# First MLP of a three-layer fused kernel: activations cast and split for two ff tiles at a time, second layer taken a pair of tiles behind

## The chip, the core and the metric

The kernel runs on one core of a Trainium2 chip. The metric is the device time of one execution in microseconds, the median of several. The engines are named as the profile names them: PE is the matrix engine (PEld its weight loads), DVE the vector engine, ACT the scalar engine, POOL the GpSimd engine, SP the engine that issues most DMAs.

## The reference

Inputs are q, k and v of shape (4, 8, 576, 64), a first MLP with d_model 512 and d_ff 1536, and a second one with d_ff 2048. Weights arrive as float64.

```python
A = sm(q, k_lm); Bm = sm(q_lm, k_lm); C = sm(q_lm, k)     # 32 landmarks, means of 18 rows
Z = ...                                                   # six Newton steps towards Bm's inverse
attn = A @ Z @ C @ v                                      # (4, 8, 576, 64) -> x of (2304, 512)
x = (sigmoid(x @ w_gate) * (x @ w_val)) @ w_out           # first MLP, d_ff 1536
h = x @ w_in                                              # second MLP, d_ff 2048
out = (max(h, 0) + alpha * min(h, 0)) @ w_out2            # (2304, 512) float32
```

## The kernel before, in words

There are four batches of 576 tokens. In each, the attention's right half (Z C v) is folded into the gate and value weights of the first MLP (`fold`, L590, and `take`, L609, make the tiles `We`), so that the first layer of the MLP multiplies the attention's left factor A directly with `We`.

Every fp32 product is made of three products of fp32r operands: an operand is split into a cast and a rest. `split` (L113) issues a cast on ACT (L115) and a subtraction, the rest, on DVE, or on POOL where asked (L116). `TERMS` (L57) lists the three products.

The first MLP works on a half batch (288 tokens, `HB`) and one ff tile (128 of 1536 columns) at a time. There are 4 x 2 x 12 = 96 such steps, walked by the loop at L756. A step calls `layer1` (L630): 6 matmuls of 288 columns into the bank gv0 (gate) and 6 into gv1 (value). ACT takes the sigmoid of gv0 into `g` (L649), DVE multiplies g by gv1 in place (L650), and `split` makes the cast and the rest of `g` in `gs` (L651). The result goes to the queue `behind` (L758). With `LAG = 2`, `catch_up` (L727) then takes the tile of two steps ago and calls `layer2` (L654): 4 output blocks of 128 columns x 3 terms = 12 matmuls of 288 columns, accumulated in four banks `acc` over a half's ff tiles. So PE's own order is: first layer of step n, second layer of step n-2, first layer of step n+1, and so on.

Where a half ends (its twelfth ff tile), the four banks are copied to four `xs` tiles, m = 0 and 2 on ACT, m = 1 and 3 on DVE (L746; in the first batch, whose halves are worked through in three segments of ff tiles, DVE adds a stored part, L744). SP stores each to DRAM (`x2d<-xs`, L748). There are eight such ends. The next half's `layer2` starts new accumulators in the same four banks.

Beside this loop run, in the same steps: conversions of the float64 weights (`narrow`, L124: ACT L130 and L134, DVE L136, L139, L142), for the second MLP from step 52 on (`narrow_w2`, L678); conversions of the stored second weights (`convert_w2`, L694); the attention of the next batches; the folds. Every engine takes its instructions in order. The framework lays that order down when the program is built, from the order of the code and its own modelled times, so instructions of neighbouring steps can change places on ACT and DVE. SP's queue also is in order: an issue that waits for a buffer holds up the issues behind it.

After step 96 the second MLP begins (L890): `layer3` (L828), and three steps later `layer4` (L850), with accumulators in the banks of `acc` and `att`. Each of its first steps also calls `catch_up` once while tiles of the first MLP are left in `behind` (L899). `store` (L862) copies a finished block into an `ob` tile, which uses the buffers of `gs`, and stores it.

Buffer counts (L63): `g` 2, `gs` (and `ob`) 4, `xs` 4.

Of the kernel before, what the change touches and what calls it, by code (L numbers as in the profile page):

```python
# [9 lines left out]
F32 = mybir.dt.float32  # L10
F32R = mybir.dt.float32r
# [10 lines left out]
def tile_landmark_attention_glu_prelu(  # L22
# [18 lines left out]
    P = 128  # L41
# [4 lines left out]
    HB = S // 2  # L46
# [5 lines left out]
    NW = 512  # L52
# [7 lines left out]
    RELOAD_AT, FOLD_AT = (16, 40), (  # L60
        (19, 20, 22, 23, 25, 27), (44, 46, 48, 50, 52, 54), (45, 47, 49, 51, 53, 55)
    )
    LAG, LAG2, G_BUFS, GS_BUFS, XS_BUFS = 2, 2, 2, 4, 4  # L63
    W2_OWN, W2_RAW = (0, 1), (29, 30, 31)
    W2_EARLY, W2_EVERY = 4, 2
    W2_FROM, W2_STEP, X2_AT = 85, 3, (11, 6)
# [6 lines left out]
    bpool = ctx.enter_context(tc.tile_pool(name="bpool", bufs=1))  # L73
# [28 lines left out]
    def f32(ap):  # L102
        return ap.bitcast(F32)
# [6 lines left out]
    def bank(name, tag="att"):  # L110
        return psp.tile([P, NW], F32, tag=tag, name=name, bufs={"att": 2, "gv": 2, "acc": 4}[tag])

    def split(dst, src, lo="dve"):  # L113

        nc.scalar.copy(dst[:, 0, :], src)  # L115
        (nc.gpsimd if lo == "pool" else nc.vector).tensor_tensor(  # L116
            out=dst[:, 1, :], in0=src, in1=f32(dst[:, 0, :]), op=ALU.subtract
        )
# [507 lines left out]
            split(We[B - 1, c, j], st, lo="pool")  # L626

    wout_sb = {}

    def layer1(b, half, f):  # L630
        c, s = divmod(f, 2)
        pss = []
        for i in range(2):
            ps = bank(f"gv{i}", "att" if b >= 2 and f % 2 else "gv")
            n = 0
            for a, e in TERMS:
                for j in range(2):
                    nc.tensor.matmul(  # L638
                        ps[:, :HB],
                        lhsT=We[b, c, j][:, a, 256 * i + P * s : 256 * i + P * s + P],  # L640
                        rhs=att[b, j, "A"][half][:, e, :],
                        start=(n == 0),
                        stop=(n == 5),
                    )
                    n += 1
            pss.append(ps)
        g = bpool.tile([P, HB], F32, tag="g", name="g", bufs=G_BUFS)
        gs = bpool.tile([P, 2, HB], F32R, tag="gs", name="gs", bufs=GS_BUFS)
        nc.scalar.activation(g, pss[0][:, :HB], AF.Sigmoid)  # L649
        nc.vector.tensor_tensor(out=g, in0=g, in1=pss[1][:, :HB], op=ALU.mult)  # L650
        split(gs, g)  # L651
        return gs

    def layer2(acc, gs, f, f0, f1):  # L654
        for m in range(NK):
# [69 lines left out]
    behind = deque()  # L725

    def catch_up():  # L727
        b, half, f, f0, f1, gs = behind.popleft()
        if f == f0:
            accs[half] = [bank(f"acc{m}", "acc") for m in range(NK)]  # L730
        layer2(accs[half], gs, f, f0, f1)
        if f < f1 - 1:
            return
        if f0 == 0 and f1 < NF1:
            part[half] = [ws_tile("part", (P, 2, HB), F32) for _ in range(2)]
        for m in range(NK):
            got, so_far = accs[half][m][:, :HB], None
            if f0 > 0 or f1 < NF1:
                so_far = part[half][m // 2][:, m % 2]
            to = so_far  # L740
            if f1 == NF1:
                to = bpool.tile([P, HB], F32, tag="xs", name="xs", bufs=XS_BUFS)
            if f0 > 0:
                nc.vector.tensor_tensor(out=to, in0=so_far, in1=got, op=ALU.add)  # L744
            else:
                (nc.vector.tensor_copy if m % 2 else nc.scalar.copy)(to, got)  # L746
            if f1 == NF1:
                nc.sync.dma_start(out=x2d[2 * b + half][:, m], in_=to)  # L748

    for b in range(B):  # L750
        if b == 0:
            segs = [(h, f0, f1) for f0, f1 in ((0, 2), (2, 6), (6, NF1)) for h in range(2)]
        else:
            segs = [(h, 0, NF1) for h in range(2)]
        order = [(h, f, f0, f1) for h, f0, f1 in segs for f in range(f0, f1)]
        for i, (half, f, f0, f1) in enumerate(order):  # L756
            at = 24 * b + i
            behind.append((b, half, f, f0, f1, layer1(b, half, f)))  # L758
            if len(behind) > LAG:
                catch_up()  # L760
            for _ in range(min(CPS, len(conv))):
                convert()
                raw_ahead(1)

            if b < 2:
                pace += ATT_PACE[b] * (at >= ATT_FROM)
                while pace >= 1:
                    next(nxt, None)
                    pace -= 1
            if at in RELOAD_AT:  # L770
                reload(0)
                reload(1)
            if at in FOLD_AT[0]:
                c = FOLD_AT[0].index(at)
                while (1, 1, "M") not in att:
                    next(nxt)
                take(1, c, fold(1, c, bank))
                reload(c + 2)
            if at in FOLD_AT[1]:
                c = FOLD_AT[1].index(at)  # L780
                for _ in nxt:
                    pass
                take(2, c, fold(2, c, bank))
            if at in FOLD_AT[2]:
                c = FOLD_AT[2].index(at)
                store_folded(c, fold(3, c, bank))
                reload(c + 2)
                if c + 1 == NCH:
                    apool.release()
                    qpool = ctx.enter_context(  # L790
                        tc.tile_pool(name="qpool", bufs=1, reuse_waits="tile")
                    )
                    rpool = tc.alloc_tile_pool(name="rpool", bufs=1, reuse_waits="tile")
            if b == 2 and half and f % 2:
                take_stored(f // 2)

            if at >= NARROW_FROM:
                narrow_pace += 1 / NARROW_EVERY
                while to_narrow and narrow_pace >= 1:
                    narrow_w2(to_narrow.popleft())  # L800
                    narrow_pace -= 1
            if qpool is not None and at > FOLD_AT[2][-1]:
                if at % W2_EVERY == 0:
                    if w2_todo and w2_todo[0] < W2_EARLY:
                        convert_w2(w2_todo.popleft())
                if at >= W2_FROM:
                    if w2_todo:
                        convert_w2(w2_todo.popleft())
# [50 lines left out]

    outv = out.rearrange("(b p r) e -> b r p e", b=B, r=R)  # L860

    def store(acc, n0, t):  # L862
        ob = bpool.tile([P, NW], F32, tag="gs", name="ob", bufs=GS_BUFS)
        (nc.vector.tensor_copy if t % 2 else nc.scalar.copy)(ob, acc)
        done = 0
        while done < P:
            bb, rem = divmod(n0 + done, S)
            r, p = divmod(rem, TP)
            step = min(P - done, TP - p)
            nc.sync.dma_start(out=outv[bb, r, p : p + step, :], in_=ob[done : done + step, :])  # L870
            done += step
# [67 lines left out]
```

## Time and profile before

| | |
|---|---|
| median of 3 runs | 899.93 us (895.19 to 902.99) |
| the profiled execution, its own time | 898.93 us |
| its span, first to last instruction | 897.1 us |
| mean granted clock of PE over the span | 0.972 of full speed |

The profile is of one execution. Busy time counts an instruction's duration on its engine; an engine's idle time before an instruction is put down to whatever released that instruction last. The first MLP's matmuls lie between 49 and 504 us of the span, the second MLP's from 495 us to the end. The granted clock has two levels, 1.2 and 2.4 GHz, shown as 0.5 and 1.

### The profile page before, as it was taken

The page shows a single profiled execution, that of the slowest core. Times are in us where ns is not written, and L with a number is a line of the kernel's source. Part 1 is how long each engine was busy: PE and PEld are TensorE (multiplying, and loading weights), DVE is VectorE, ACT ScalarE, POOL GpSimd, SP SyncE. Part 2 cuts the span into 40 slices and gives each one's busy share as a digit, 9 for nine tenths or more (in the row PEclk, how much of TensorE's full clock was granted, in tenths as well). Part 3 has the DMA queues.
Part 4 walks back from the last instruction along what each step waited for, and adds up shares of the span by engine and source line. Part 5 has one row for each costly group of instructions (what it writes and reads, how often), then busy time and mean ns, then how long its engine had stood idle before and what let it go on. Part 6 is the DMA issues. An engine that isn't in the chain of part 4 may idle for free.

```text
span 897.1 us, 15129 instructions
## 1 busy us (share of the span) xinstructions
PE 853.4 (95%) x5969; PEld 710.7 (79%) x5969; DVE 508.9 (57%) x1005; ACT 337.1 (38%) x711; POOL 92.4 (10%) x90
## 2 busy tenths in 40 slices
PE   5689889999999999998999999999999999999997
PEld 4357667877887877998999888888888888888896
DVE  3789998565565343778766664444344333443443
ACT  6666865354364333555555431121121111111111
POOL 0131112110011000133200020110010001000000
PEclk9679999999999999998999999999999999999999
DMA  9776778734331242888876530020002000100100
GB/s 248 247 221 177 253 240 257 216 115 135 81 104 49 94 145 94 271 282 253 265 250 194 153 86 21 16 78 1 1 24 58 1 1 13 48 0 1 31 18 24
DMA packets 85160, 106.92 MB, mean 119 GB/s; under 512 B 35664, under 2 KB 57184, under 8 KB 85088
## 3 DMA queue, kind: packets, MB, share of 16 engines
q1 hardware_dynamic: 81632, 93.36, 34.7%
q0 software_dynamic: 3456, 12.58, 4.5%
q8 instruction: 47, 0.77, 0.4%
q14 instruction: 25, 0.20, 0.1%
HBM read 78.65 MB, written 27.26 MB: 118 GB/s over the span
## 4 chain that ended last, share of the span: by engine, by line
PE 84%; DVE 6%; DMA 5%; issue 2%; ACT 2%; POOL 1%; SPq 0%; DVEq 0%; ACTq 0%
PE h L834 22%; PE o L852 22%; PE gv L638 15%; PE acc L657 14%; PE psf L600 4%; DMA raw<-in_moe_w_out_dram 2%; PE psq L191 2%; DMA raw<-in_moe_w_in_dram 1%; PE psc L210 1%; DVE raw L139 1%; PE psz L403 1%; PE psa L210 1%; DMA tk<-in_k_dram 1%; PE psv L314 1%; DMA tkT<-in_k_dram 1%
## 5 line engine op out<-in xcount | busy, mean ns | idle before, releaser
L638 PE MATMUL gv<-A,we 128*128 128x288 f32 x1152 | 197.8, 312 | 6.0 <-ACT g L649 3.4
L638 PEld LDWEIGHTS gv<-A,we 128*128 128x128 f32 x1152 | 167.1, 196 | 36.8 <-issue 25.6
L657 PE MATMUL acc<-gs,wconv 128*128 128x288 f32 x1152 | 184.5, 304 | 8.8 <-DVE xs L746 3.5
L834 PE MATMUL h<-x,w 128*128 128x512 f32 (+1 forms) x840 | 183.8, 368 | 0.0
L657 PEld LDWEIGHTS acc<-gs,wconv 128*128 128x128 f32 x1152 | 163.8, 192 | 20.8 <-issue 6.8
L852 PE MATMUL o<-w,g2s 128*128 128x512 f32 x702 | 170.0, 390 | 0.0
L834 PEld LDWEIGHTS h<-x,w 128*128 128x128 f32 x840 | 148.1, 188 | 27.2
L852 PEld LDWEIGHTS o<-w,g2s 128*128 128x128 f32 x702 | 130.9, 188 | 26.6
L115 ACT CAST g2s<-g 128x512 fp32r<-128x512 f32 (+1 forms) x80 | 46.3, 578 | 269.3 <-DVE g L844 269.3
L840 DVE TENSOR_SCALAR g<-h,alphaT 128x512 f32<-128x512 f32 (+1 forms) x80 | 55.8, 697 | 148.6 <-PE h L834 148.5
L116 DVE TENSOR_TENSOR g2s<-g,g2s 128x512 fp32r<-128x512 f32 (+1 forms) x80 | 55.7, 696 | 55.1 <-ACT g2s L115 54.5
L650 DVE TENSOR_TENSOR g<-g,gv 128x288 f32<-128x288 f32 x96 | 43.1, 449 | 39.2 <-PE gv L638 38.0
L649 ACT ACTIVATE g<-gv 128x288 f32<-128x288 f32 x96 | 39.5, 411 | 66.1 <-PE gv L638 62.9
L116 DVE TENSOR_TENSOR gs<-g,gs 128x288 fp32r<-128x288 f32 x96 | 52.0, 541 | 21.2 <-ACT gs L115 20.9
L115 ACT CAST gs<-g 128x288 fp32r<-128x288 f32 x96 | 41.5, 432 | 50.7 <-DVE g L650 50.4
L116 POOL TENSOR_TENSOR x<-xr,x 128x512 fp32r<-128x512 f32 (+1 forms) x20 | 23.9, 1206 | 314.1 <-ACT x L115 313.9
L139 DVE SCALAR_TENSOR_TENSOR raw<-raw 128x512 uint32<-128x512 uint32 x68 | 47.6, 711 | 13.0 <-ACT raw L134 12.2
L130 ACT ACTIVATE raw<-raw 128x512 f32<-128x512 f32 x68 | 46.2, 681 | 21.9 <-DMA raw<-in_moe_w_out_dram 9.5
L844 DVE SCALAR_TENSOR_TENSOR g<-h,g 128x512 f32<-128x512 f32 (+1 forms) x80 | 51.0, 638 | 2.6
L600 PE MATMUL psf<-wgv,m 64*32 64x512 f32 x384 | 43.4, 625 | 0.4 <-DVE m L469 0.2
L116 DVE TENSOR_TENSOR we<-psf,we 128x512 fp32r<-128x512 f32 x36 | 23.6, 686 | 18.6 <-ACT we L115 18.5
L115 ACT CAST we<-psf 128x512 fp32r<-128x512 f32 x36 | 19.8, 588 | 29.6 <-PE psf L600 29.5
(129 smaller groups left out, 735.1 us busy)
## 6 DMA issues: line engine op xcount, KB each, us to landing
raw<-in_moe_w_out_dram SPq DMA_DIRECT2D x28, 512.0 KB, 4.9
wgv<-wgvd POOLq DMA_DIRECT2D x24, 512.0 KB, 4.6
raw<-in_moe_w_in_dram SPq DMA_DIRECT2D x16, 512.0 KB, 3.9
w2d<-n SPq DMA_DIRECT2D x32, 256.0 KB, 2.6
st<-w2d SPq DMA_DIRECT2D x32, 256.0 KB, 2.9
raw<-in_moe_w_gate_dram SPq DMA_DIRECT2D x24, 256.0 KB, 4.6
raw<-in_moe_w_val_dram SPq DMA_DIRECT2D x24, 256.0 KB, 4.9
wgvd<-wgv SPq DMA_DIRECT2D x12, 512.0 KB, 5.6
```

The lines of the kernel that those rows point to most:

```text
L115: nc.scalar.copy(dst[:, 0, :], src)
L116: (nc.gpsimd if lo == "pool" else nc.vector).tensor_tensor(out=dst[:, 1, :], in0=src, in1=f32(dst[:, 0, :]), op=ALU.subtract)
L130: nc.scalar.activation(w[:, :, 1], w[:, :, 1], AF.Copy, scale=2.0 ** -112)
L139: nc.vector.scalar_tensor_tensor(out=lo, in0=hi, scalar=0x80000000, in1=lo, op0=ALU.bitwise_and, op1=ALU.bitwise_or)
L600: nc.tensor.matmul(pss[j][LM * h : LM * h + LM], lhsT=att[b, j, "M"][d, u], rhs=wgv[c, j][d, u], start=True, stop=True,)
L638: nc.tensor.matmul(ps[:, :HB], lhsT=We[b, c, j][:, a, 256 * i + P * s : 256 * i + P * s + P], rhs=att[b, j, "A"][half][:, e, :], start=(n ...
L650: nc.vector.tensor_tensor(out=g, in0=g, in1=pss[1][:, :HB], op=ALU.mult)
L657: nc.tensor.matmul(acc[m][:, :HB], lhsT=wout_sb[f][:, a, P * m : P * m + P], rhs=gs[:, e, :], start=(f == f0 and n == 0), stop=(f == f1 - ...
L834: nc.tensor.matmul(ps[:, :n], lhsT=w[:, a, kk], rhs=xs[:, e, kk, :n], start=(i == 0), stop=(i == 11))
L840: nc.vector.tensor_scalar(out=g[:, :n], in0=ps[:, :n], scalar1=0.0, scalar2=alphaT[:, f : f + 1], op0=ALU.min, op1=ALU.mult,)
L844: nc.vector.scalar_tensor_tensor(out=g[:, :n], in0=ps[:, :n], scalar=0.0, in1=g[:, :n], op0=ALU.max, op1=ALU.add)
L852: nc.tensor.matmul(acc, lhsT=gs[:, a, P * t : P * t + P], rhs=w2_out[f][:, e, :], start=(f == 0 and i == 0), stop=(f == NF2 - 1 and i == 2),)
```

## The change

`g` becomes a tile for two ff tiles. Sigmoid and product still run once per ff tile, each into its half. After the second tile of a pair, one `split` makes cast and rest of 576 columns into one `gs` tile of both. `layer1` therefore returns nothing at an even tile and two entries at an odd one, so that the second layer of a step is that of three steps ago, and three entries instead of two are left when the first MLP's loop ends. The buffer counts become `g` 2 (of twice the size), `gs` 2 (of twice the size), `xs` 3. Two `ob` tiles of the final store share one `gs` buffer.

```diff
-    LAG, LAG2, G_BUFS, GS_BUFS, XS_BUFS = 2, 2, 2, 4, 4
+    LAG, LAG2, G_BUFS, GS_BUFS, XS_BUFS = 2, 2, 2, 2, 3
...
+    both = [None]
...
-        g = bpool.tile([P, HB], F32, tag="g", name="g", bufs=G_BUFS)
-        gs = bpool.tile([P, 2, HB], F32R, tag="gs", name="gs", bufs=GS_BUFS)
+
+        if s == 0:
+            both[0] = bpool.tile([P, 2, HB], F32, tag="g", name="g", bufs=G_BUFS)
+        g = both[0][:, s]
         nc.scalar.activation(g, pss[0][:, :HB], AF.Sigmoid)
         nc.vector.tensor_tensor(out=g, in0=g, in1=pss[1][:, :HB], op=ALU.mult)
-        split(gs, g)
-        return gs
+        if s == 0:
+            return []
+        gs = bpool.tile([P, 2, 2, HB], F32R, tag="gs", name="gs", bufs=GS_BUFS)
+        split(
+            gs.rearrange("p a s t -> p a (s t)"), both[0].rearrange("p s t -> p (s t)")
+        )
+        return [(f - 1, gs[:, :, 0]), (f, gs[:, :, 1])]
...
-            behind.append((b, half, f, f0, f1, layer1(b, half, f)))
+            behind.extend((b, half, ff, f0, f1, gs) for ff, gs in layer1(b, half, f))
             if len(behind) > LAG:
                 catch_up()
...
+    out_tiles = [None]
+
     def store(acc, n0, t):
-        ob = bpool.tile([P, NW], F32, tag="gs", name="ob", bufs=GS_BUFS)
+        if t % 2 == 0:
+            out_tiles[0] = bpool.tile([P, 2, NW], F32, tag="gs", name="ob", bufs=GS_BUFS)
+        ob = out_tiles[0][:, t % 2]
```

## Rows read from the trace of the kernel before

**Rows 1.** The page's first part: busy time of each engine.

```profile
PE 853.4 (95%) x5969; PEld 710.7 (79%) x5969; DVE 508.9 (57%) x1005; ACT 337.1 (38%) x711; POOL 92.4 (10%) x90
```

**Rows 2.** By stretch: busy PE, PEld, DVE, ACT, POOL; granted clock, DMA share, GB/s.

```profile
50.00:200.00 150.00, 140.94 (x1258) 106.33 (x1258) 122.19 (x271) 91.83 (x198) 28.51 (x29) 0.96 0.72 212
...
350.00:500.00 150.00, 143.58 (x1023) 140.16 (x1022) 106.95 (x186) 80.39 (x170) 23.45 (x16) 0.95 0.74 239
```

**Rows 3.** What PE waited for, whole span: us in total, times, longest.

```profile
PE acc L657 <- DVE xs L746: 3.5, 3, 1.9
PE gv L638 <- ACT g L649: 3.4, 3, 2.3
PE acc L657 <- ACT xs L746: 3.0, 2, 2.3
...
PE acc L657 <- DVE gs L116: 2.1, 2, 1.6
```

**Rows 4.** Busy time by stretch around the three waits for xs; columns as in rows 2.

```profile
376.00:386.00 10.00, 8.62 (x53) 8.62 (x54) 7.42 (x14) 4.92 (x12) 2.63 (x3) 0.83 0.91 270
418.00:428.00 10.00, 8.14 (x38) 7.80 (x39) 7.65 (x15) 4.49 (x11) 1.26 (x1) 0.66 0.93 281
461.00:469.00 8.00, 6.37 (x33) 5.78 (x33) 6.65 (x14) 4.97 (x13) 0.00 (x0) 0.79 0.73 216
```

**Rows 5.** Groups by form, ACT casts and DVE rests of 288 and 576 columns.

```profile
L116 DVE TENSOR_TENSOR gs<-g,gs 128x288 fp32r<-128x288 f32 x96 | 52.0, 541 | 21.2 <-ACT gs L115 20.9
...
L115 ACT CAST gs<-g 128x288 fp32r<-128x288 f32 x96 | 41.5, 432 | 50.7 <-DVE g L650 50.4
...
L115 ACT CAST A<-at 128x576 fp32r<-128x576 f32 x6 | 4.1, 676 | 5.1 <-DVE at L362 5.1
...
L116 DVE TENSOR_TENSOR A<-at,A 128x576 fp32r<-128x576 f32 x4 | 3.0, 757 | 0.7 <-ACT A L115 0.7
...
L116 DVE TENSOR_TENSOR A<-at,A 128x288 fp32r<-128x288 f32 x4 | 1.7, 451 | 0.0
```

**Rows 6.** Timeline of an undisturbed step, third batch: start, duration, what, idle before.

```profile
357.35 1.74 PE L638 MATMUL gv<-A,we 128*128 128x288 f32 x12
...
360.15 0.46 DVE L116 TENSOR_TENSOR gs<-g,gs 128x288 fp32r<-128x288 f32 x1 [0.50 <-ACT gs L115]
...
365.29 0.95 PE L657 MATMUL acc<-gs,wconv 128*128 128x288 f32 x6
```

**Rows 7.** Timeline where a half of the third batch ends.

```profile
373.89 0.43 ACT L746 COPY xs<-acc 128x288 f32<-128x288 f32 x1
...
375.43 1.52 DVE L116 TENSOR_TENSOR gs<-g,gs 128x288 fp32r<-128x288 f32 x1
...
375.78 2.86 SPq L748 DMA_DIRECT2D x2d<-xs  x4
...
377.38 1.46 PE L657 MATMUL acc<-gs,wconv 128*128 128x288 f32 x9 [1.95 <-DVE xs L746]
```

**Rows 8.** The same where the third batch itself ends.

```profile
418.53 0.43 ACT L115 CAST gs<-g 128x288 fp32r<-128x288 f32 x1 [0.43 <-DVE g L650]
418.87 0.39 ACT L746 COPY xs<-acc 128x288 f32<-128x288 f32 x1
...
420.60 2.58 PE L657 MATMUL acc<-gs,wconv 128*128 128x288 f32 x9 [0.55 <-DVE xs L746]
```

**Rows 9.** DMAs of tile xs; the issue of 419.28 alone; that of 461.89 alone.

```profile
DMA to landing us min/median/max: 1.7/3.9/6.6
x2d<-xs SPq DMA_DIRECT2D x1, 144.0 KB, 3.8
x2d<-xs SPq DMA_DIRECT2D x1, 144.0 KB, 1.7
```

**Rows 10.** Timeline where the second MLP begins.

```profile
502.20 1.78 PE L657 MATMUL acc<-gs,wconv 128*128 128x288 f32 x12
...
505.48 0.81 DVE L746 COPY xs<-acc 128x288 f32<-128x288 f32 x2
```

## The prediction

> **What bounds the kernel now.** I read the page's busy line first, because it says which engine can set the end. PE is busy for 853.4 of 897.1 us [rows 1]; its work is untouched by this change, which alters ACT, DVE and buffers alone. So the question is where PE waits for those two. The table by stretch comes next [rows 2]. From 50 to 200 us PE is busy for 140.9 of 150 us, with DVE at 122.2 and ACT at 91.8. From 350 to 500 it has 6.4 us of idle time, at DVE 107 and ACT 80. From 500 on PE runs the second MLP, which this change leaves as it is but for its first steps.
>
> The list of waits names the causes [rows 3]: 3.4 us for the sigmoid, 2.1 us for the rest of `gs`, and 3.5 + 3.0 = 6.5 us for the copies `xs` out of the four accumulators. These last are the whole idle time of the third stretch. They lie at three places, the ends of halves near 377, 419 and 462 us. After each, the granted clock falls to its lower level for a time [rows 4]: a mean of 0.83 over 10 us is 3.4 us at 1.2 GHz, 0.66 is 6.8 us, 0.79 over 8 us is 3.4 us. That is 13.6 us at half speed, which costs about 6.8 us. So the three places together cost some 13 us, and from 50 to 200 us PE is idle for 150 - 140.9 = 9 us, of which 5.5 us are the waits for the sigmoid and the rest.
>
> **The change, part by part.**
>
> *One cast and one rest for two tiles.* The 96 casts of 432 ns become 48. A cast of 576 columns is in the trace, at 676 ns, so a pair saves 2 x 432 - 676 = 188 ns, or 9.0 us of ACT in all. The rest of 576 columns took 757 ns. Against two of 451 ns (undisturbed) a pair saves 145 ns; against two of the mean 541 it saves 325 ns. That is 7 to 16 us of DVE [rows 5]. Half or more of it falls where PE hardly waits, and of the saving from 50 to 200 us (some 13 pairs: 2.4 us of ACT, 1.9 to 4.2 us of DVE) only what shortens a queue that PE waits for counts. PE's idle time there is 9 us [rows 2], ended by these two engines in 5.5 us at the least [rows 3]. DVE's load falls by 2 to 3%, and since a queue that is nearly full shortens by more than its load, I give 13% of the 9 us back: -1.2 us. Bounds: -9 if all goes, and +1.5 if the longer instructions make the five waits of these two rows longer by 0.31 us each (757 - 451).
>
> *The second layer a pair behind.* Before, the rest of tile f is wanted after four blocks: second layer of f-2, first of f+1, second of f-1, first of f+2. After, from the odd tile's first layer to the even tile's second layer there are again four blocks, and six to the odd one's. From 357.35 to 365.29 there are five blocks, so a block is 1.59 us. In this undisturbed step the rest ends at 360.61 and its first reader starts at 365.29, so 4.7 us are to spare [rows 6]. Cast and rest of a pair end (676 - 432) + (757 - 451) = 0.55 us later. I cost this at 0; the cover is those 4.7 us, and if a late queue eats them each pair costs up to 0.55 us. The two `gs` buffers are free when wanted: the last reader of the pair before last stands one first-layer block, 1.59 us, ahead.
>
> *One more block of lag.* The first second-layer block starts one step later at the head, and three blocks instead of two are left for the second MLP. PE's sum is the same. If PE were starved at the head the moved block would cost its 1.59 us; from 50 to 200 us PE is idle for 6% only [rows 2], so I take +0.3 (0 to 1.6).
>
> *The accumulators at the end.* Before, the last second-layer block starts at 502.20 and the copies on DVE end at 506.29 [rows 10], beside a block of `layer3`. After, that block comes a step later and directly ahead of the first `layer4`, which wants two of the four banks. The copies' 4.1 us from the block's start, less the block's 1.6, are then uncovered if nothing is put between: 0 to 2.5 us. The other two accumulators of that step use other banks and another `layer3` stands ready, so I take +0.5.
>
> *Three xs tiles.* The fourth copy (m = 3, DVE) must now wait until the store of m = 0 has landed. Behind it on DVE stand the narrowing of weights, the rest of a converted weight and the next product; behind those wait ACT's cast, the free raw buffers and so SP's next loads. On an ideal schedule the block that ends a half starts at B, the copy of m = 0 is done at about B + 1.0 (three matmuls, 0.4, and the copy, 0.43), and the next half reaches its fourth accumulator at B + 2 x 1.59 + 1.19 (nine of twelve matmuls) = B + 4.37. So 4.37 - 1.0 - 0.45 = 2.9 us are there for issue and landing. The median landing is 3.9, the range 1.7 to 6.6 [rows 9]. In the first two batches folds and attention matmuls stand between the blocks and PE waited for no xs copy [rows 2, 3], so I count no place there. At the last end the fourth copy has no reader near. Three places remain:
>
> - 377 us: the first store is issued at 375.78, 1.46 us after its copy, since SP's queue was held [rows 7]; it landed about 3.8 us later, at 379.6. The fourth copy would end at 380.1 and its three matmuls at 380.5 or so, where the block ended at 378.84: +1.7.
> - 419 us: copied at 418.87, landed 3.8 us after the issue of 419.28, at 423.1. The block would end at about 424.1 instead of 423.18: +1.0 [rows 8, 9]. But the step in which a half ends is an even one now (the twelfth tile's second layer comes at the third step of the next half), and even steps have no cast and no rest. Here the copy stood behind a `gs` cast that itself waited 0.43 us for DVE's product [rows 8]. Without the cast, and with DVE's queue lighter by one rest, I take 1.6 us off: -0.6.
> - 462 us: landed after 1.7, before the fourth copy ran anyway: 0.
>
> Sum +1.1. Bounds: -13.3 if the lighter step takes the waits and the low clock away (6.5 + 6.8), and 3 x (6.6 - 2.9) = +11.1 with the longest landing at each place, issued at once.
>
> Two rules of the Trainium skill are weighed against this. The rows have DVE busy for 57% and ACT for 38% of the span [rows 1], and what they cost PE are waits in their queues [rows 3]. "Perfetto Trace Analysis", section on optimizing Scalar and DVE operations, says that grouping helps where the engine is saturated, but that where these engines are not and still cause bubbles on others, breaking instructions up may finish work sooner; by that the change goes the wrong way, which is the third rival below. The store's landing took 3.8 us at two of the three places [rows 9]. "DMA: Bandwidth & Descriptors", section on the anatomy of a DMA, gives about 2.0 us of fixed time; with that, 377 would add nothing, and the sum would be about -1.0 us.
>
> *The rest* (`ob` pairs, `g` of twice the size): a block's stores lie far apart, no wait of PE hangs on them, 0.
>
> Sum: -1.2 + 0 + 0.3 + 0.5 + 1.1 = +0.7 us against the profiled execution's 898.93, so 899.6. The median of the runs lies 1.0 above that execution, so I name 900.5.
>
> **Rivals.**
>
> 1. *Slower: the third xs buffer decides.* Where the store's issue is held as at 377 us and the landing takes 3.8, the fourth copy comes 5.3 us after the first, against the 2.9 that are covered; it decides once issue and landing pass 2.9. If all three places pay the 1.7 of 377 (5.1), the low clock lasts 6.8 us instead of 3.4 at two of them (2 x 1.7 = 3.4), and the end pays its 2.5, the sum is +11: 911. For it: the loads of SP stand ahead of the stores, and the DMA share there is 0.73 to 0.93 [rows 4]. Against it: at 462 the landing took 1.7, and the waits already there would be replaced, not added to.
> 2. *Faster: the lighter step ends the waits at the halves.* If the copies run as soon as their matmuls end, 6.5 us of waits and 6.8 of clock go, of which the store's landing gives part back. Half of it is -6.6: 893; all of it 887. For it: at 419 the cast stood in front of the copy, and at 377 a rest of `gs` of 1.52 us stood in front of DVE's copies [rows 7, 8]. Against it: the landing of the first store replaces the wait, and the narrowing of weights stays in the same queues.
> 3. *Bursts: the longer cast and rest hold up the sigmoid and the product.* In the first two batches the next first layer wants the banks back one block later. ACT is held 0.24 us longer and DVE 0.31 us longer at every second step. With the five waits of today it is +1.5 in place of -1.2, 2.7 over the forecast: 903; with all 24 pairs of those batches it is 24 x 0.31 = 7.4: 908. For it: PE's wait for the sigmoid is the longest of its kind today, 3.4 us [rows 3]. Against it: the two engines have less work in all.
>
> That the saving is hidden entirely lies inside the forecast: then the time is that of before.
>
> **How the numbers follow.** The forecast, between -3 and +4 us of before, gets 0.50; the first rival 0.18, the second 0.20, the third 0.12. A measurement of this kernel can tell about 1% from no change, 9 us. Below 891 lies a little less than half of the second rival: 0.09. Above 909 lies some two thirds of the first: 0.12. The rest, 0.79, is within. The range from 891 to 909 leaves out those two tails. Cases of both signs hold much of the chance; the forecast's own range is 897 to 904.
>
> **What would show it.** Groups by form should show 48 casts near 676 ns and 48 rests near 757 to 900 ns, and about 9 us less of ACT. The list of waits should show `acc <- xs` waits at the three places again, ended now by DVE's fourth copy, with the store's landing as that copy's own releaser, and still 2 to 4 us together more or less than 6.5. The granted clock should fall again near the same ends of halves. The sigmoid and `gs` waits up to 200 us should sum to about 8 us. I would be wrong if the waits for xs pass 10 us or vanish, if a new wait for `gs` appears in the second batch, or if the second MLP's first steps lose more than 2.5 us.

## The result, and the profile after

The changed kernel takes 907.91 us (median of 4 timed executions, 907.0 to 911.84) beside 898.76 us for the kernel before (895.19 to 902.99): a ratio of 1.0100, with a 95% interval of 1.0061 to 1.0139 (below, such an interval stands in brackets behind its ratio). It is slower, by about the 9 us that this measurement can just tell from no change. The profiled execution took 908.52 us with a span of 906.5 us, 9.4 us more than the 897.1 of before. In the listings below L639 is the matmul of `layer1`, L665 that of `layer2`, L754 and L756 the copies `xs` and their stores, L842 and L860 the matmuls of `layer3` and `layer4` (before: L638, L657, L746, L748, L834, L852).

The engines' part of the page, which answers to [rows 1], and the groups by form, which answer to [rows 5]:

```profile
PE 853.2 (94%) x5969; PEld 706.6 (78%) x5969; DVE 499.8 (55%) x957; ACT 329.9 (36%) x663; POOL 92.9 (10%) x90
```

```profile
L116 DVE TENSOR_TENSOR gs<-g,gs 128x576 fp32r<-128x576 f32 x48 | 37.2, 776 | 16.9 <-ACT gs L115 16.7
L115 ACT CAST gs<-g 128x576 fp32r<-128x576 f32 x48 | 32.3, 672 | 29.7 <-DVE g L653 28.4 <-PE acc L665 1.2
```

The change does what it says. ACT gives up 41.5 - 32.3 = 9.2 us of casts and DVE 52.0 - 37.2 = 14.8 us of rests. PE is as busy as before, and its idle time grew from 43.7 to 53.3 us (span less busy time). The equal sum hides something: up to the ninth block of `layer3` PE's busy time falls from 498.05 to 492.70 us, and from there to the end it grows from 355.36 to 360.49.

PE's waits, which answer to [rows 3] (us in total, times, longest), and the granted clock around the ends of halves, which answers to [rows 4] (the clock is third from the end):

```profile
PE acc L665 <- DVE xs L754: 7.9, 4, 3.7
PE gv L639 <- ACT g L652: 5.7, 5, 2.5
PE acc L665 <- ACT xs L754: 4.6, 2, 3.8
...
PE acc L665 <- DVE gs L116: 1.4, 3, 1.0
```

```profile
373.00:385.00 12.00, 8.28 (x59) 7.61 (x58) 10.11 (x16) 5.54 (x12) 2.01 (x2) 1.00 0.79 261
419.00:429.00 10.00, 8.18 (x41) 8.10 (x42) 6.98 (x14) 6.00 (x12) 3.65 (x2) 0.66 0.90 294
462.00:477.00 15.00, 11.23 (x62) 10.79 (x63) 8.52 (x17) 6.39 (x12) 0.00 (x0) 0.77 0.81 273
```

The waits for xs are 12.5 us where they were 6.5. The clock falls to its lower level at two of the three places, for 6.8 us each (a mean of 0.66 over 10 us, 0.77 over 15): 13.6 us in sum, as before. But 6 us more of waits are not 9.4. The table by stretch shows where the rest is: first the stretch from 540 us of the kernel before, then that of the one after, with the two that answer to [rows 2] ahead of it:

```profile
540.00:890.00 350.00, 350.00 (x1635) 293.49 (x1634) 148.04 (x224) 51.71 (x92) 13.12 (x12) 1.00 0.07 19
```

```profile
50.00:200.00 150.00, 136.26 (x1238) 103.38 (x1237) 120.28 (x252) 88.81 (x183) 27.52 (x28) 0.97 0.69 210
350.00:500.00 150.00, 138.32 (x981) 135.84 (x981) 99.92 (x162) 75.95 (x148) 24.35 (x16) 0.95 0.75 240
540.00:890.00 350.00, 350.00 (x1597) 288.73 (x1596) 145.23 (x215) 50.69 (x90) 13.14 (x12) 1.00 0.07 19
```

From 350 to 500 us PE is idle for 11.7 us, where it was 6.4. From 540 on, in the second MLP, which the change touches only in its first steps, PE has no idle time in either kernel, at a full clock, and does 1597 matmuls where it did 1635 (part of this difference is that the short matmuls at the end are reached later). Is each matmul slower? Here are the ninth and the eightieth block of `layer3` in the timeline (start, duration), before and after:

```profile
536.47 1.30 PE L834 MATMUL h<-x,w 128*128 128x512 f32 x5
...
886.13 1.11 PE L834 MATMUL h<-x,w2r 128*128 128x256 f32 x8
```

```profile
540.66 1.09 PE L842 MATMUL h<-x,w 128*128 128x512 f32 x4
...
895.41 1.36 PE L842 MATMUL h<-x,w2r 128*128 128x256 f32 x10
```

It is 4.2 us behind at the ninth block and 9.3 at the eightieth, so 5.1 us are lost between: this stretch takes 354.75 us in place of 349.66. The groups by form of the stretch from 560 to 860 us say which matmuls are slower (the last number ahead of the bar's 0.0 is the mean of one in ns), before and after:

```profile
L834 PE MATMUL h<-x,w 128*128 128x512 f32 x533 | 128.1, 389 | 0.0
L852 PE MATMUL o<-w,g2s 128*128 128x512 f32 x531 | 127.9, 389 | 0.0
...
L852 PE MATMUL o<-w2x,g2s 128*128 128x512 f32 x42 | 10.2, 390 | 0.0
L834 PE MATMUL h<-x,w2x 128*128 128x512 f32 x36 | 8.6, 389 | 0.0
```

```profile
L842 PE MATMUL h<-x,w 128*128 128x512 f32 x541 | 133.4, 394 | 0.0
L860 PE MATMUL o<-w,g2s 128*128 128x512 f32 x528 | 127.5, 390 | 0.0
...
L860 PE MATMUL o<-w2x,g2s 128*128 128x512 f32 x36 | 8.9, 395 | 0.0
L842 PE MATMUL h<-x,w2x 128*128 128x512 f32 x36 | 8.7, 390 | 0.0
```

`layer3` is slower with weights `w`, not with `w2x`; `layer4` is slower with `w2x`, not with `w`. From start to start a `layer3` matmul with weights `w` takes 229 and 237 ns by turns, 232.7 on average, in place of 227. What tells these apart is where the two operands lie. `x2` and `w2x` are in pools allocated behind `bpool`, `w` and `g2s` are not. The change makes `bpool` larger by two tiles `g` of 1152 bytes per partition and smaller by one `xs` of 1152, so everything behind it lies 1152 = 4 x 256 + 128 bytes higher. The slow matmuls are those of which one operand moved and the other didn't.

### The profile page after: what moved, and what is told of

It is laid out like the page before. It is cut to its first block, busy times and chain, and to the rows that moved or that the text cites. A ratio compares the mean times of both kernels' runs of the same rounds, so it can differ in the third digit from the quotient of the medians.

```text
span 906.5 us, 15024 instructions
## 1 busy us (share of the span) xinstructions
PE 853.2 (94%) x5969; PEld 706.6 (78%) x5969; DVE 499.8 (55%) x957; ACT 329.9 (36%) x663; POOL 92.9 (10%) x90
## 4 chain that ended last, share of the span: by engine, by line
PE 72%; DMA 11%; DVE 8%; ACT 3%; issue 3%; SPq 1%; POOL 1%; DVEq 0%; ACTq 0%; POOLq 0%
PE o L860 22%; PE h L842 21%; PE gv L639 10%; PE acc L665 9%; DMA raw<-in_moe_w_out_dram 4%; PE psf L600 3%; DMA st<-w2d 2%; DVE raw L139 2%; PE psq L191 2%; DMA st<-we3d 1%; DMA x2d<-xs 1%; PE psc L210 1%; DMA raw<-in_moe_w_in_dram 1%; PE psv L314 1%; DVE n L142 1%
## 5 line engine op out<-in xcount | busy, mean ns | idle before, releaser
L639 PE MATMUL gv<-A,we 128*128 128x288 f32 x1152 | 195.9, 309 | 10.4 <-ACT g L652 5.7
L665 PE MATMUL acc<-gs,wconv 128*128 128x288 f32 x1152 | 183.2, 303 | 13.9 <-DVE xs L754 7.9
L639 PEld LDWEIGHTS gv<-A,we 128*128 128x128 f32 x1152 | 164.5, 192 | 40.5 <-issue 24.1
L842 PE MATMUL h<-x,w 128*128 128x512 f32 (+1 forms) x840 | 187.9, 372 | 0.0
L665 PEld LDWEIGHTS acc<-gs,wconv 128*128 128x128 f32 x1152 | 163.8, 192 | 25.0 <-DVE xs L754 9.1
L842 PEld LDWEIGHTS h<-x,w 128*128 128x128 f32 x840 | 148.1, 188 | 30.6
L860 PE MATMUL o<-w,g2s 128*128 128x512 f32 x702 | 171.0, 391 | 0.0
L860 PEld LDWEIGHTS o<-w,g2s 128*128 128x128 f32 x702 | 130.9, 188 | 28.1
L139 DVE SCALAR_TENSOR_TENSOR raw<-raw 128x512 uint32<-128x512 uint32 x68 | 49.6, 741 | 19.3 <-ACT raw L134 18.1
L852 DVE SCALAR_TENSOR_TENSOR g<-h,g 128x512 f32<-128x512 f32 (+1 forms) x80 | 51.0, 638 | 2.7
L116 DVE TENSOR_TENSOR gs<-g,gs 128x576 fp32r<-128x576 f32 x48 | 37.2, 776 | 16.9 <-ACT gs L115 16.7
L115 ACT CAST gs<-g 128x576 fp32r<-128x576 f32 x48 | 32.3, 672 | 29.7 <-DVE g L653 28.4
L600 PE MATMUL psf<-wgv,m 64*32 64x512 f32 x384 | 40.4, 620 | 1.2 <-DVE wgv L142 0.7
```

Source lines behind the costliest of these rows:

```text
L116: (nc.gpsimd if lo == "pool" else nc.vector).tensor_tensor(out=dst[:, 1, :], in0=src, in1=f32(dst[:, 0, :]), op=ALU.subtract)
L139: nc.vector.scalar_tensor_tensor(out=lo, in0=hi, scalar=0x80000000, in1=lo, op0=ALU.bitwise_and, op1=ALU.bitwise_or)
L600: nc.tensor.matmul(pss[j][LM * h : LM * h + LM], lhsT=att[b, j, "M"][d, u], rhs=wgv[c, j][d, u], start=True, stop=True,)
L639: nc.tensor.matmul(ps[:, :HB], lhsT=We[b, c, j][:, a, 256 * i + P * s : 256 * i + P * s + P], rhs=att[b, j, "A"][half][:, e, :], start=(n ...
L665: nc.tensor.matmul(acc[m][:, :HB], lhsT=wout_sb[f][:, a, P * m : P * m + P], rhs=gs[:, e, :], start=(f == f0 and n == 0), stop=(f == f1 - ...
L842: nc.tensor.matmul(ps[:, :n], lhsT=w[:, a, kk], rhs=xs[:, e, kk, :n], start=(i == 0), stop=(i == 11))
```

## The experiments

**The addresses alone.** The theory: a distance of an odd multiple of 128 bytes between the two operands costs 5 us. The rival: the second MLP is slower because it begins in another order or because of the pairs of output tiles. In the kernel before the move is made without the change, in the changed kernel it is taken back:

```diff
-                to = bpool.tile([P, HB], F32, tag="xs", name="xs", bufs=XS_BUFS)
+                to = bpool.tile([P, HB + 8], F32, tag="xs", name="xs", bufs=XS_BUFS)[:, :HB]
```

> The kernel before with its four xs tiles 32 bytes per partition wider, so that everything allocated behind the pool, x2 and w2x of the second MLP among it, lies 128 bytes higher; nothing else differs and no instruction moves. Theory (addresses): the two xs waits explain only part of the 9.4 us, the rest is lost in the second MLP because the larger pool moved x2 and w2x by an odd multiple of 128 bytes against the weights; then the layer3 matmuls take 234 ns from start to start instead of 227, a step of the second MLP takes 5.53 us instead of 5.44, and the span is 5.4 us longer than before, about 902.5. Rival (the second MLP runs slower because it begins in another order, with the last second layer directly ahead of it, or because of the pairs of output tiles): 227 ns, 5.44 us and the span of before within 1 us.

```diff
-    out_tiles = [None]
+    out_tiles = [None, bpool.tile([P, 32], F32, tag="pad", name="pad", bufs=1)]
```

> The changed kernel with one unused tile of 128 bytes per partition at the end of the pool, so that x2 and w2x lie at the same remainder of 256 bytes as in the kernel before. Theory (addresses): the layer3 matmuls go back to 227 ns and a step of the second MLP to 5.44 us, and the span falls by about 5.4 us, from 906.5 to 901; what stays of the loss, some 4 us, lies in the first MLP, at the waits for xs. Rival (order at the start of the second MLP, or output pairs): no gain, about 906.5.

Groups by form in the same stretch, of the first and then of the second:

```profile
L834 PE MATMUL h<-x,w 128*128 128x512 f32 x536 | 132.1, 394 | 0.0
```

```profile
L842 PE MATMUL h<-x,w 128*128 128x512 f32 x540 | 129.7, 389 | 0.0
```

128 bytes alone give the kernel before the 394 ns of the changed one, a span of 902.5 us (+5.4, as expected) and a ratio of 1.0045 [1.0017, 1.0073]. Taken back in the changed kernel, they give 389 ns, a span of 899.8 (-6.7) and a ratio to before of 1.0036 [1.0005, 1.0067] in place of 1.0100. The spans hold what else differs between two profiles; the stretch from the ninth to the eightieth `layer3` block doesn't. It takes 354.75 us with the 128 bytes alone and 349.66 with them taken back, to the hundredth what it takes in the changed kernel and in the one before. The theory stands in both directions. Two more kernels ask how far it goes: 64 bytes at the end of the pool, and 64 bytes in front of everything, so that all tiles move together.

```diff
     outv = out.rearrange("(b p r) e -> b r p e", b=B, r=R)
+
+    pad = bpool.tile([P, 16], F32, tag="pad", name="pad", bufs=1)
```

> The kernel before with an unused tile of 64 bytes per partition at the end of the pool: x2 and w2x lie 64 bytes higher against the weights in place of 128. If any difference of the two start addresses within 256 bytes slows TensorE: 228 to 234 ns from start to start in layer3 and a span 2 to 6 us longer. If only the 128 does: 227 ns and the span of before within 2 us.

```diff
     cpool = ctx.enter_context(tc.tile_pool(name="cpool", bufs=1))
+    pad = cpool.tile([P, 16], F32, tag="pad", name="pad", bufs=1)
```

> The kernel before with an unused tile of 64 bytes at the very start, so that every tile, the weights too, lies 64 bytes higher and all differences between tiles stay. If the pace depends on how the addresses of what is read together stand to each other: 227 ns in layer3 and layer4 and the span of before within 3 us. If it depends on each address by itself: 229 to 234 ns and a span 4 to 6 us longer in the second MLP.

Groups by form of the kernel with 64 bytes between, then of the one with all tiles moved (its edit adds a line, so `layer3` is L835 there):

```profile
L834 PE MATMUL h<-x,w 128*128 128x512 f32 x546 | 133.2, 392 | 0.0
L852 PE MATMUL o<-w,g2s 128*128 128x512 f32 x528 | 129.0, 393 | 0.0
```

```profile
L835 PE MATMUL h<-x,w 128*128 128x512 f32 x528 | 126.8, 389 | 0.0
```

A common move costs nothing (349.66 us for the same stretch, span 894.4), so it is the distances that count. A distance of 64 costs too (354.34 us), and there `layer4` with `w` and `g2s` is slow though neither of them moved. So it isn't only the two operands of one matmul; which other access takes part there stays open.

**The third xs buffer alone**, on the kernel before, with wider tiles so that no address changes:

```diff
-    LAG, LAG2, G_BUFS, GS_BUFS, XS_BUFS = 2, 2, 2, 4, 4
+    LAG, LAG2, G_BUFS, GS_BUFS, XS_BUFS = 2, 2, 2, 4, 3
...
-                to = bpool.tile([P, HB], F32, tag="xs", name="xs", bufs=XS_BUFS)
+                to = bpool.tile([P, HB + 96], F32, tag="xs", name="xs", bufs=XS_BUFS)[:, :HB]
```

> The kernel before with three xs buffers in place of four, each widened so that the pool and every address behind it stay as they were. Theory (the third xs buffer makes the longer waits of the first MLP): the fourth copy waits for the landing of the first store, PE's waits for xs grow from 6.5 us to 9 to 13, and the span is 2 to 5 us longer than before, with the second MLP's steps at 5.44 us. Rival (the waits for xs grew because of the pairs, whose cast and rest now stand elsewhere): xs waits and span of before within 1 us.

In the view of the tile xs: the idle time of the engine ahead of the copies, by what ended it, and what PE waited.

```profile
  DMA x2d<-xs: 6.6, 3
...
  PE acc L657: 6.9, 6
```

Copies do wait for stores, 6.6 us at three places, but PE's waits for xs are 6.9 us beside 6.5. The ratio is 1.001 [0.9982, 1.0037]. The span of the one profiled execution, 901.6, is what the theory expected; the ten timed ones say that the buffer alone changes the time by -1.6 to +3.3 us. By itself it explains at most 3.3 of the 9 us.

**The order alone**: the kernel before, single tiles, second layer three tiles behind.

```diff
-    LAG, LAG2, G_BUFS, GS_BUFS, XS_BUFS = 2, 2, 2, 4, 4
+    LAG, LAG2, G_BUFS, GS_BUFS, XS_BUFS = 3, 2, 2, 4, 4
```

> The kernel before with the second layer three tiles behind in place of two: casts and rests of single tiles, four xs buffers, all addresses as before; only the order of the second-layer blocks is that of the changed kernel. Theory (the last second-layer block now stands directly ahead of the first layer4, whose banks wait for the copies of the accumulators): layer4 waits 0.7 to 3.7 us for xs as in the changed kernels, and the fifth layer3 of the second MLP starts 1 to 4 us later than before; the span is 1 to 4 us longer, 898 to 901. Rival (the wait there comes of the pairs): no wait at layer4, span within 1 us of before.

The ratio is 1.008 [1.0047, 1.0114], the span 908.7: worse than expected. The timeline where the second MLP begins, and the clock of that stretch (0.57):

```profile
514.10 0.62 ACT L115 CAST w<-st 128x512 fp32r<-128x512 f32 x1 [0.81 <-DMA st<-w2d]
514.62 0.39 ACT L746 COPY xs<-acc 128x288 f32<-128x288 f32 x1
...
515.07 1.22 PE L852 MATMUL o<-w2x,g2s 128*128 128x512 f32 x2 [3.15 <-ACT xs L746]
```

```profile
513.00:521.00 8.00, 5.88 (x14) 4.18 (x15) 5.85 (x10) 3.26 (x7) 0.00 (x0) 0.57 0.69 195
```

The last block of the second layer (510.13, 1.78 us long) ends at 511.9. The copy of its first accumulator stands on ACT behind casts of the second MLP's weights that wait for their loads, and runs at 514.62. `layer4`, directly behind that block now, waits 3.15 us, and the clock falls to its lower level for 6.8 us, which costs another 3.4.

**Pairs with four xs buffers**, one `g` of a pair in place of two, so that the pool has its old size:

```diff
-    LAG, LAG2, G_BUFS, GS_BUFS, XS_BUFS = 2, 2, 2, 2, 3
+    LAG, LAG2, G_BUFS, GS_BUFS, XS_BUFS = 2, 2, 1, 2, 4
```

> The changed kernel with one g buffer of a pair in place of two and four xs buffers in place of three: the pool has the size of before, and x2 and w2x their addresses. Theory (the third xs buffer and the addresses make the whole loss): no copy of xs waits for a store, the xs waits of PE are 6.5 us or less, the second MLP's steps take 5.44 us, and the span is that of before or up to 3 us shorter, 894 to 898. Rival (bursts: the longer cast and rest hold up the sigmoid and the product, or the one g buffer does): PE's waits for the sigmoid, the product and gs grow from some 8 us, and the span is 2 to 7 us longer than before, 899 to 904.

The xs waits of the halves are 5.9 us and the layer3 pace is that of before, as expected, but the ratio is 1.0071 [1.0045, 1.0097] and the span 907.0, above what either side expected. `layer4` waits 3.6 us for the ACT copy of xs and the clock falls behind it, as in the run above. The waits for sigmoid, product and `gs` sum to 2.2 + 3.3 + 3.3 = 8.8 us. They are 9.1 in the changed kernel and 5.5 in the one before, so the rival's bursts are there too: 3.3 us, beside the 3.6 of `layer4` and the 3.4 that the low clock behind it costs.

**Mending one cost after the other** in the changed kernel. First, beside the 128 bytes, two second-layer blocks in the second MLP's second step, so that a `layer3` stands between the last of them and `layer4`:

```diff
-        if behind:
+        for _ in range(min(len(behind), 1 + (f == 1))):
             catch_up()
```

> The changed kernel with the 128 bytes of filling, and two of the three left second-layer blocks in the second step of the second MLP, so that a layer3 block of 2.7 us stands between the last of them and the first layer4, as before the change. Theory: the waits of layer4 for xs (1.3 us in the profile without this) go, and the span is 1 to 2 us shorter than without, 898 to 899. Rival (the copies were late for another reason, the casts of the second MLP's weights in ACT's queue): the wait stays near 1 us or moves to the second of the two blocks, whose gs is not ready, and the span is 899.8 as without.

The wait at `layer4` is gone. Span 894.7, ratio 1.0004 [0.9971, 1.0036]. So the ratio goes from 1.0100 to 1.0036 with the bytes taken back, and to 1.0004 with the last blocks moved as well; the intervals of these last two overlap, so this second part is likely, not settled. Then a buffer of tag "A" for the fourth copy, so that no copy of the third and fourth batch waits for a store:

```diff
-                to = bpool.tile([P, HB], F32, tag="xs", name="xs", bufs=XS_BUFS)
+                if b >= 2 and m == 3:
+                    to = bpool.tile([P, HB], F32, tag="A", name="xs4", bufs=4)
+                else:
+                    to = bpool.tile([P, HB], F32, tag="xs", name="xs", bufs=XS_BUFS)
```

> The one with the second MLP's second step doubled, and in the third and fourth batch the copy of the fourth accumulator goes to a buffer of the folded activations that is free by then, so that no copy waits for a store at 377, 419 and 462 us. Theory (the third xs buffer makes the longer waits there): no copy of an accumulator is released by a store's landing at these places, PE's waits for xs fall from 11 us to 5 to 7, the span falls by 3 to 6 us to 893 to 896, and with it the kernel is 0 to 0.5% faster than before. Rival (the waits at the halves come of the order of the queues on ACT and DVE, whichever buffer is used): waits of 9 us or more, span 897 to 900.

PE's waits from 320 to 480 us, of the one without the buffer and the one with it (where the copy `xs` is L757):

```profile
PE acc L665 <- DVE xs L754: 5.8, 4, 2.1
PE acc L665 <- ACT xs L754: 4.7, 2, 4.2
PE acc L665 <- DVE gs L116: 0.6, 1, 0.6
```

```profile
PE acc L665 <- DVE gs L116: 3.8, 3, 1.9
PE acc L665 <- ACT xs L757: 2.2, 4, 1.4
PE acc L665 <- DVE xs L757: 1.5, 2, 1.1
```

The waits for xs fall from 10.5 to 3.7 us, more than expected, and 3.2 us of it come back at once as waits for `gs`; in this profile `layer4` waits 2.4 us again, although a `layer3` stands between. The ratio is 0.998 [0.9955, 1.0004]: the fastest of these kernels, but not told from the one before. The profiled span, 897.3, is the rival's.

Then no weights of the second MLP are converted until the accumulators are copied:

```diff
-        w2_pace += W2_STEP
+        w2_pace += W2_STEP * (not behind)
```

> The combination of the run before it, and the second MLP converts none of its weights until the last accumulators of the first MLP are copied. Theory (there the first copy of xs stood on ACT behind casts of weights that waited for their loads, layer4 waited 2.35 us for it and the granted clock fell for 3.4 us): no wait of layer4 for xs and no low clock there, the fifth layer3 starts 3 to 5 us earlier than in the combination, the span is 892 to 894, and the kernel is 0.3 to 0.8% faster than before. Rival (the casts put off are wanted soon after, or the low clock comes anyway): the wait goes to a layer3 for its weights w, span 896 to 898.

This missed: ratio 1.0000 [0.9968, 1.0032], and `layer4` still waits 1.2 us. The edit didn't take the casts out of the copy's way. By the code, 15 of the 32 conversions of these weights are called for in the first MLP's steps; yet 23 of their casts run on ACT ahead of the copy, in this kernel as in the one before it. So the order that the framework lays down put eight of the postponed ones in front again, and what the copy costs without them stays open. Last, the same order with single tiles, on the kernel before:

```diff
-    LAG, LAG2, G_BUFS, GS_BUFS, XS_BUFS = 2, 2, 2, 4, 4
+    LAG, LAG2, G_BUFS, GS_BUFS, XS_BUFS = 3, 2, 2, 4, 4
...
-        if behind:
+        for _ in range(min(len(behind), 1 + (f == 1))):
             catch_up()
...
-        w2_pace += W2_STEP
+        w2_pace += W2_STEP * (not behind)
```

> The kernel before, casts and rests of single tiles, with the second layer three tiles behind, two second-layer blocks in the second step of the second MLP, and no weights converted there until the accumulators are copied: the same order as the run beside it, without pairs. If the pairs give something once their costs are taken away, this is slower than the run with pairs by 1 to 6 us (9.2 us of ACT and 14.8 us of DVE are what pairs save, off the path for the most part). If they give nothing: within 1 us of it. Either way layer4 doesn't wait for xs, and the fifth layer3 starts within 21 us of the first.

The ratio is 1.0033 [1.0006, 1.0059], so the kernel with pairs looks 0.33% better, 3 us, in the same order. The intervals of the two runs overlap: likely, not settled. It also has more room for `g`, which is taken up below.

## Why the prediction was right or wrong

The time, 907.9, lies inside the range, near its upper end, but 7.4 us above the 900.5 named, and it is slower where the forecast was no change. That it lies inside is luck: some 5 us of the loss come from a term that stood in the sum at 0. The milestones of the two profiles divide the 9.4 us (the changed kernel runs one second-layer block later, so up to the second MLP it owes 1.75 us more). Up to the third batch the changed kernel is 4.6 us ahead (its first block of that batch starts at 310.15 in place of 316.53), in the third and fourth it loses 7.1, from the first to the ninth `layer3` block 3.5 less the owed 1.75, and behind that 5.2.

**"The rest (`ob` pairs, `g` of twice the size): ... no wait of PE hangs on them, 0."** This is the step that failed. No wait does hang on them, but the larger `g` moved the second MLP's operands by 128 bytes and every step there takes 5.53 us in place of 5.44. That is 5.1 to 5.4 us in the profiles, and between 1.5 and 6.6 in the timed runs of the one that moves addresses alone. I asked of each edit what waits for it, and of none where it puts the other tiles. No row of before could have priced it, but an open place in the sum belonged there.

**Three xs tiles, +1.1.** The term was mis-sized: the xs waits are 6.0 us longer. (In the prediction, the -1.0 beside the Trainium skill's 2.0 us takes the late landing away at 377 alone; away at 419 too, the sum would be -2.0. The section named there is on DMAs issued from GpSimd. These stores are issued by SP, and they landed after 1.7 to 6.8 us here.) The timeline of the four places:

```profile
326.14 0.46 DVE L754 COPY xs<-acc 128x288 f32<-128x288 f32 x1 [3.46 <-DMA x2d<-xs]
...
326.65 0.53 PE L665 MATMUL acc<-gs,wconv 128*128 128x288 f32 x2 [1.27 <-DVE xs L754]
...
379.68 0.67 PE L665 MATMUL acc<-gs,wconv 128*128 128x288 f32 x3 [2.35 <-DVE xs L754]
...
419.81 0.68 ACT L130 ACTIVATE raw<-raw 128x512 f32<-128x512 f32 x1 [1.46 <-DMA raw<-in_moe_w_out_dram]
...
420.39 0.38 ACT L754 COPY xs<-acc 128x288 f32<-128x288 f32 x1
...
420.82 2.62 PE L665 MATMUL acc<-gs,wconv 128*128 128x288 f32 x9 [3.81 <-ACT xs L754]
...
467.94 0.43 DVE L136 TENSOR_SCALAR raw<-raw 128x512 uint32<-128x512 uint32 x1 [1.12 <-DMA raw<-in_moe_w_out_dram]
468.40 0.46 DVE L754 COPY xs<-acc 128x288 f32<-128x288 f32 x1
...
468.91 1.09 PE L665 MATMUL acc<-gs,wconv 128*128 128x288 f32 x3 [3.71 <-DVE xs L754]
```

- 326 us, which I dismissed ("I count no place there"): the fourth copy waits 3.46 us for a store. PE loses 1.27.
- 377, [rows 7]: waits of 0.77, 0.61 and 2.35 us in place of 1.95, so +1.8; I had +1.7. The cause is another, though: this first store was issued at 374.03 and landed after 2.2 us, long before the copy of 379.18, which had stood behind a narrowing and the product in DVE's queue.
- 419, [rows 8]: 3.81 in place of 2.85. I had taken 1.6 us off for the cast that is no longer in front of the copy. It is gone, and a narrowing that waited for its load stands there instead.
- 462, [rows 9]: 3.71 in place of 1.63, where I had 0. The first store landed 6.3 us after its issue of 462.11, where it took 1.7 before; at the same time DVE's queue was held by a narrowing that waited for its load.

So DVE's fourth copy held by the store's landing, the sign I had named, is there at 326, undecided at 462 (landing and queue end together at 468.37), and absent at the other two. The missing buffer lies behind the longer waits all the same: with pairs and three buffers they are 10.5 to 12.5 us in three kernels, with a fourth 3.7 to 5.9 in three. How it makes them where no copy waits for a landing isn't shown. My own bound for being wrong, xs waits over 10 us, is passed; the other, 2.5 us lost in the second MLP's first steps, isn't (1.7). That these waits are worth less than their length is seen from the experiment with the extra buffer, which took 6.8 us of them away for 0.24% of the time (2.2 us, with intervals that overlap).

**One cast and one rest, -1.2.** The durations came as read: 672 against 676 ns, 776 against 757. But [rows 3] answers the other way than the term supposed: up to 200 us PE's waits for the sigmoid, the product and the rest sum to 5.7 + 2.0 + 1.0 = 8.7 us, near the 8 that I had named as a sign, where they were 5.5. The first two batches gained 4.6 us in the profile all the same. Of these 2.05 us are a wait for a load of k (204.79 us of the kernel before) that is absent here, and 1.7 one stretch of low clock less.

The gain isn't of one profile, however. The third batch begins at 308.5 to 311.8 us in the five kernels with pairs and two buffers `g`, at 314.7 to 322.8 in the seven with single tiles, and at 318.8 in the one with pairs and one `g`. The block that is taken later, 1.75 us, does not make up for that. So it seems to go with the second `g` of a pair, which makes room for four tiles where there was room for two, and not with the fewer casts and rests. The timed comparisons in one order agree: with two `g`, 1.0036 beside 1.008 (with three xs buffers against four) and 1.0000 beside 1.0033, 3 to 4 us in favour of pairs, with intervals that overlap; with one `g`, 1.0071 beside 1.008, under 1 us. Single tiles with four `g` were not run, so what pairs are worth by themselves, and whether the term's -1.2 has the right sign, stays open.

**The second layer a pair behind, 0.** Right. A steady step of the third batch, for [rows 6]:

```profile
349.14 0.76 DVE L116 TENSOR_TENSOR gs<-g,gs 128x576 fp32r<-128x576 f32 x1 [0.74 <-ACT gs L115]
...
354.33 1.74 PE L665 MATMUL acc<-gs,wconv 128*128 128x288 f32 x12
```

The rest ends at 349.90 and its first reader, three blocks on, starts at 354.33: 4.4 us to spare, where there were 4.7.

**One more block of lag, +0.3, and the accumulators at the end, +0.5.** The bounds of the second, 0 to 2.5, took the copies to run at once. The timeline where the second MLP begins, for [rows 10]:

```profile
507.37 1.76 PE L665 MATMUL acc<-gs,wconv 128*128 128x288 f32 x12
...
510.07 0.62 ACT L115 CAST w<-st 128x512 fp32r<-128x512 f32 x1 [1.03 <-DMA st<-w2d]
510.59 0.39 ACT L754 COPY xs<-acc 128x288 f32<-128x288 f32 x1
...
511.04 2.12 PE L860 MATMUL o<-w2x,g2s 128*128 128x512 f32 x8 [0.75 <-ACT xs L754]
```

ACT's second copy stands behind a cast that waits for its load; that queue was not counted, although the same pair of lines stands in the kernel before, where ACT's copy ends after those on DVE:

```profile
505.69 0.62 ACT L115 CAST w<-st 128x512 fp32r<-128x512 f32 x1 [1.51 <-DMA st<-w2d]
506.22 0.39 ACT L746 COPY xs<-acc 128x288 f32<-128x288 f32 x1
```

It costs 0.75 us here, 3.15 and 3.6 with a fall of the clock in two other kernels. "PSUM — Partial Sum Buffer" of the Trainium skill, section on engine and sequencer instructions, calls the queues of ScalarE and VectorE strictly first in, first out; the trace agrees (the copy of 510.59 starts only behind the cast of 510.07), and I applied it at the halves and not here. Order and lag alone cost 0.8%, with the end mended 0.33%.

**The rivals.** The third buffer alone makes at most 3.3 us, so it isn't the main cause, though its time of 911 came near. The lighter step did not end the waits. The bursts are there: the waits for sigmoid, product and `gs` sum to 7.6 to 15.5 us in the six kernels with pairs and to 5.5 to 7.2 in the seven with single tiles. They don't decide the time by themselves, for the kernel with the lowest ratio, 0.998, has 14.1 us of them.

## What to carry to other kernels

An edit that changes a buffer's size moves everything allocated behind it: count the bytes, and try the old remainders with an unused tile before blaming the edit. Ask of every late copy what else stands in its engine's queue waiting for a load, and leave a block of other work between the last write of an accumulator and the reuse of its bank; here it ended the wait in two kernels of four. Count the room in buffers apart from the number of instructions, when one edit changes both. A single profile here strays by several us in the first MLP; compare timed ratios, and use the profile for where.

## What the hardware showed that was not expected

PE's pace depends on where tiles lie to each other. A matmul of 512 columns starts 227 ns after the one before it in the kernel before and with all tiles moved by 64 bytes. With 128 bytes between its operands, the distances in `layer3` are 229 and 237 ns by turns; with 64 bytes, the medians are 227 to 231 by group. From 560 to 860 us PE had no idle time and a full clock in all of these kernels.

At 128 bytes the other engines aren't the reason. Of the changed kernel's `layer3` matmuls with weights `w` in that stretch, 426 run while DVE, ACT and POOL all rest, and these start 233.3 ns apart on average; 387 such matmuls of the kernel before start 226.7 ns apart. "SBUF — State Buffer" of the Trainium skill, section on the two sides, says that among the engines only the port pair shared by VectorE and GpSimd causes contention, and that PE never waits on anyone. Matmuls that are slow beside resting engines don't contradict it; yet the pace changes with the addresses, by 1.7% of a step of the second MLP (5.44 to 5.53 us). Whether PE's own two reads, the moving operand and the next weights, get in each other's way is not shown.
